# Local attention and a two-layer feed-forward on one core: one written order for units 16 to 127, seven products from unit 20 on, and relu slopes split between ScalarE and VectorE

## The chip, the cores and the metric

The kernel runs on 1 core of one Trainium2 chip. The metric is the device time of one execution in microseconds (us); three runs of the kernel before gave 884.85, 886.47 and 890.36, median 886.47.

## What is computed

Attention with a window of 32 positions and 32 global tokens, 8 batches of 8 heads, 512 local positions, head size 64; its output, 4608 tokens of 512 numbers, goes through a feed-forward of 2048 hidden units with a slope for negative values:

```python
s_g = scale * q_g @ concat(k_g, k_l).T;  out_g = softmax(s_g) @ concat(v_g, v_l)
s_l = concat(scale * q_l @ k_g.T, where(|i - j| <= 32, scale * q_l @ k_l.T, -1e9))
out_l = softmax(s_l) @ concat(v_g, v_l)
x = concat(out_g, out_l) as (4608, 512)
h = x @ w_in                                   # 512 -> 2048
g = maximum(h, 0) + alpha * minimum(h, 0)      # alpha of 2048
return g @ w_out                               # 2048 -> 512
```

## The kernel before

The tokens are nine groups: eight local ones of 512 tokens (one a batch) and one of the 256 global tokens. The hidden layer is cut into 16 blocks of 128. A unit t = 16 G + f is block f of group G: a first product (x by block f of w_in, into a PSUM bank h_ps), the slopes, and, two units later (LAG), the second product (g by block f of w_out, into four banks o). All 32-bit operands are split into an upper part (a cast on ScalarE: xh, gh, wt) and a lower part (a subtraction: xl, gl), and each product is three matmuls, so that a unit of a local group has twelve matmuls of 512 columns in its first product and twelve in its second. Attention is computed beside it, 32 head pairs P, four steps s each, one step a unit: s = 0 local scores (s_ps) and softmax, s = 1 a transpose of the probabilities p through DRAM (transpose_q, fetch_pt), s = 2 values (o_ps and g_ps, two banks), global scores and global softmax, s = 3 the global part's transpose. Group G needs head pairs 4G to 4G + 3.

Units 0 to 15 (begin, line 996) follow an order that a planner at build time writes from costs and due times (early, line 159). The change leaves it alone.

From unit 16 on the loop at the end of longformer_ffn sets the order, in three forms:
- Units 16 to 29 (slow_unit): plain products; ScalarE, VectorE and GpSimd aren't pinned, so the framework's scheduler may move their instructions. CATCH (line 45) gives units 16, 23 and 30 two steps of attention instead of one.
- Units 30 and 31 (border_units): pinned, written out.
- Units 32 to 127 (fast_unit): pinned, "seven products". For two blocks f and f + 1 and the two halves of the tokens, f1_fast (line 831) takes seven products of 256 columns instead of eight, with sums of the weights (weight_sums, line 396: s24, s3 and a changed part of wt) and sums of x (x_sums, line 735, and x_last for group 7: b11, b12, b21, b22 are the quarters of x, t1 to t4 their sums). Four products stand in the even unit, three in the odd one; VectorE then adds the parts (u<-u,h_ps and h_ps<-u,h_ps). The third product of the odd unit reads t4.

The x sums of a group are made at the end of the group before, at the places (f, where) in X_STEPS (line 46); the last step, which makes t4, stands in the group's first unit. The weight sums are made once for each pair q of blocks; six of the eight stand in units 18 to 28, the last two in units 29 and 33.

The slopes of a local unit in units 16 to 127 are two instructions on VectorE (slopes, line 903: g = min(h, 0) alpha, then max(h, 0) + g), but for the last pair of a group (added and both), where ScalarE takes relu(-h) (negatives, line 887) and VectorE adds beta times it to h (add_slopes, line 892), with beta = 1 - alpha (line 1023). Then ScalarE casts gh and GpSimd makes gl.

Banks: h_ps has two buffers, and the attention's s_ps, o_ps and g_ps share two. global_bank (line 556) clears a corner of the g_ps bank with a memset on VectorE before TensorE may write there. Instructions on one engine run in their written order.

Of the kernel before, what the change touches and what calls it, by code (L numbers as in the profile page):

```python
# [7 lines left out]
F32 = mybir.dt.float32  # L8
# [26 lines left out]
HP = 50  # L35
NPRE = 19
# [266 lines left out]
def longformer_ffn(ctx: ExitStack, tc: tile.TileContext, qk, v, w, alpha, out):  # L303
# [82 lines left out]
    def load_out_weights(T):  # L386
        wos[T] = wpool.tile([128, 2, 512], F32R, tag="w", name="wo")
        sync.dma_start(wos[T].bitcast(F32), wod[T % NF])
# [342 lines left out]

    def less(o, a, b):
        vec.tensor_tensor(o, a, b, op=ALU.subtract)

    def x_sums(G, step):
        if step == 0:
            upper(G, "b11", b11)
            lower(G, "b11", b11, vec)
            less(b11, b12, b11)
        if step == 1:  # L740
            less(b12, b22, b12)
        if step == 2:
            upper(G, "t1", b11)
            upper(G, "t3", b12)
# [17 lines left out]
    def x_last(step):  # L762

        G = NB - 1
        if step == 0:
            upper(G, "b11", b11)
            lower(G, "b11", b11, vec)
            less(b11, b12, b11)
            less(b12, b22, b12)
        if step == 1:  # L770
            spare("t2")
            upper(G, "t1", b11)
            upper(G, "t3", b12)
            lower(G, "t1", b11, vec)
        if step == 2:
            less(b11, b22, b11)
            lower(G, "t3", b12, vec)
        if step == 3:
            upper(G, "t2", b11)
            upper(G, "b22", b22)  # L780
            upper(G, "b21", b21)
            lower(G, "t2", b11, vec)
        if step == 4:
            lower(G, "b22", b22, pool)
            lower(G, "b21", b21, vec)
        if step == 5:
            less(b21, b21, b11)
            upper(G, "t4", b21)
            lower(G, "t4", b21, pool)

    def prepare(t, at):
        G, f = divmod(t, NF)
        if f:
            G += 1
        if G == NB - 1 and (f, at) in LAST_STEPS:
            x_last(LAST_STEPS.index((f, at)))
        if G * NF not in FAST or (f, at) not in X_STEPS:
            return
        if G < NB - 1:
            x_sums(G, X_STEPS.index((f, at)))  # L800
# [24 lines left out]
    def product(dst, w, x, start):  # L825
        for c in range(2):
            for j, e in ((0, 0), (1, 0), (0, 1)):
                matmul(dst, w[:, j, 128 * c : 128 * c + 128], x[e][:, 256 * c : 256 * c + 256], start=start, stop=not start, skip_group_check=True)
                start = False

    def f1_fast(T):
        G, f = divmod(T, NF)
        q = f // 2
# [28 lines left out]
        def even():  # L862
            vec.tensor_tensor(h0[:, hi], u[:, lo], h0[:, hi], op=ALU.add)
            prelu(T - 1, h0, SL)

        def odd():
            vec.tensor_tensor(h1[:, lo], u[:, lo], h1[:, lo], op=ALU.add)
            prelu(T, h1, SL)

# [13 lines left out]
        if f == NF - 1:  # L883
            return added, both
        return even, odd
# [6 lines left out]
    def add_slopes(T, g, h):  # L892
        f = T % NF
# [9 lines left out]
    def slopes(T, h, n):  # L903
        f = T % NF
# [73 lines left out]

    def values(P, first):
        last = gpart.pop(P)  # L980
        if live(P - 1):
            ob = bank(first, "o_ps")
            pv_all(P - 1, ob, last)
        if live(P):
            global_scores(P)
        if live(P - 1):
            pv_out(P - 1, ob, last)
# [127 lines left out]
    def attn(u, where):  # L1115
        P, s = divmod(u, 4)
        if not (live(P) or live(P - 1)):
            return
        if (s, where) == (0, "pre") and live(P):
            local_scores(P)  # L1120
        if s < 2 and where == "pre" and live(P):
            part = softmax(P, s)
            part["red"]()
            part["ex"]()
            tails.extend(part[k] for k in ("rza", "rzr", "nm"))
        if where == "mid":
            while tails:
                tails.pop(0)()
        if (s, where) == (2, "mid"):
            gpart[P] = global_bank(P)  # L1130
            values(P, "s")
            if live(P):
                load_v(P)
        if not live(P):
            return
        if (s, where) == (2, "post"):
            global_softmax(P)
            if live(P + 2):
                load_qk(P + 2)
        if P >= NRAW:  # L1140
            if (s, where) == (2, "pre") and (P, 0) not in scratch:
                transpose_q(P, 0)
            if u == NPRE + 2 * NF + len(CATCH) - 1 and where == "post":
                transpose_q(P, 0)
            if (s, where) == (3, "pre") and P > 8:
                fetch_pt(P, 0)
                transpose_q(P, 1)
# [203 lines left out]
```

## Time and profile before

| what | value |
|---|---|
| median of three runs | 886.47 us |
| the profiled execution | 887.61 us |
| its span, first to last instruction | 885.8 us |
| granted TensorE clock | 1.0 |
| TensorE busy (matmuls) | 866.2 us, 98% |
| VectorE busy | 616.3 us, 70% |
| ScalarE busy | 392.7 us, 44% |
| GpSimd busy | 323.9 us, 37% |

The page names the engines PE (TensorE), DVE (VectorE), ACT (ScalarE), POOL (GpSimd) and SP (SyncE). A share is a mean over stages; a matmul's end is modelled, so the time that TensorE takes is read from the distance between starts. Nearly every instruction stands under one line, 294 or 323, since two helpers record them all; tiles tell them apart.

### The profile page before, as it was taken

How to read it: one execution, taken by the hardware profiler on the slowest of the kernel's cores; microseconds unless marked ns; L12 is line 12 of the kernel's file. 1: busy time of each engine (PE TensorE's matmuls, PEld its weight loads, DVE VectorE, ACT ScalarE, POOL GpSimd, SP SyncE). 2: the span in 40 equal slices, each digit the busy share in tenths (PEclk: the TensorE clock that was granted, in tenths of full speed). 3: DMA queues.
4: the chain of work that ended last, by engine and by line, in shares of the span. 5: the costliest groups of instructions: out<-in, count | busy, mean ns of one | idle time of the engine just before them, and what ended most of it. 6: DMA issues, size and time to landing. Idle time of an engine off the chain costs nothing.

```text
span 885.8 us, 22467 instructions
## 1 busy us (share of the span) xinstructions
PE 866.2 (98%) x8678; PEld 751.2 (85%) x8678; DVE 616.3 (70%) x1690; ACT 392.7 (44%) x1162; POOL 323.9 (37%) x281
## 2 busy tenths in 40 slices
PE   7799999999999999999999999999999999999998
PEld 5677777878888888888898888888898898889898
DVE  7999999976767667666676667666676656455432
ACT  7898885544444334432354334432354324211221
POOL 4455443655434332423243332423243323222222
PEclk9999999999999999999999999999999999999999
DMA  9879997977457766776657666776657553645630
GB/s 357 343 256 387 335 336 251 324 247 236 152 180 220 250 214 220 263 241 232 211 173 254 211 215 217 255 250 231 212 184 250 173 185 95 215 168 169 220 134 25
DMA packets 80906, 201.23 MB, mean 227 GB/s; under 512 B 21280, under 2 KB 41248, under 8 KB 77088
## 3 DMA queue, kind: packets, MB, share of 16 engines
q1 hardware_dynamic: 80800, 199.80, 66.1%
q8 instruction: 69, 1.13, 0.5%
q14 instruction: 37, 0.30, 0.1%
HBM read 160.96 MB, written 38.80 MB: 226 GB/s over the span
## 4 chain that ended last, share of the span: by engine, by line
PE 73%; DVE 14%; DMA 6%; ACT 4%; issue 2%; POOL 1%; SPq 1%; DVEq 0%; ACTq 0%; POOLq 0%
PE o L323 34%; PE h_ps L323 30%; PE o_ps L323 4%; PE s_ps L323 3%; DVE wt L294 2%; PE g_ps L323 2%; DVE wsum L294 2%; DVE p L294 2%; DVE g L294 2%; ACT p L294 2%; DVE wraw L294 1%; DMA pt<-scratch 1%; DMA scratch<-p 1%; DMA v<-in_v_dram 1%; DMA wa<-wt 1%
## 5 line engine op out<-in xcount | busy, mean ns | idle before, releaser
L294 POOL TENSOR_TENSOR gl<-g,gh 128x512 fp32r<-128x512 f32 (+1 forms) x128 | 161.4, 1263 | 368.0 <-ACT gh L294 270.4
L323 PE MATMUL o<-gh,wo 128*128 128x512 f32 (+1 forms) x1024 | 244.4, 380 | 0.0
L323 PE MATMUL h_ps<-xh,wt 128*128 128x256 f32 (+1 forms) x1024 | 222.4, 310 | 2.2 <-DVE g L294 1.3
L294 ACT CAST gh<-g 128x512 fp32r<-128x512 f32 (+1 forms) x144 | 85.9, 597 | 289.0 <-DVE g L294 288.3
L323 PEld LDWEIGHTS o<-gh,wo 128*128 128x128 f32 x1024 | 176.7, 188 | 32.1 <-issue 0.4
L323 PEld LDWEIGHTS h_ps<-xh,wt 128*128 128x128 f32 x1024 | 166.2, 188 | 20.5 <-issue 4.0
L323 PE MATMUL h_ps<-xl,wt 128*128 128x256 f32 (+1 forms) x512 | 157.4, 307 | 0.0
L323 PE MATMUL o<-gl,wo 128*128 128x512 f32 (+1 forms) x512 | 131.2, 377 | 0.0
L294 DVE TENSOR_SCALAR g<-h_ps,alpha_sb 128x512 f32<-128x512 f32 (+1 forms) x116 | 82.5, 712 | 39.0 <-PE h_ps L323 33.6
L323 PEld LDWEIGHTS o<-gl,wo 128*128 128x128 f32 x512 | 92.8, 188 | 18.5
L294 POOL TENSOR_TENSOR p<-p,rz 128x512 f32<-128x512 f32 x64 | 70.7, 1121 | 96.2 <-DVE rz L294 93.4
L323 PEld LDWEIGHTS h_ps<-xl,wt 128*128 128x128 f32 x512 | 96.1, 188 | 5.1
L294 DVE TENSOR_TENSOR h_ps<-u,h_ps 128x256 f32<-128x256 f32 x144 | 61.1, 425 | 50.6 <-PE h_ps L323 48.7
L294 ACT ACTIVATE p<-p,mn 128x128 f32<-128x128 f32 x224 | 86.9, 396 | 5.1 <-DVE mn L294 4.9
L323 PE MATMUL h_ps<-xh,s 128*128 128x256 f32 x480 | 88.6, 280 | 0.4 <-DVE h_ps L294 0.2
L294 DVE TENSOR_TENSOR u<-u,h_ps 128x256 f32<-128x256 f32 x96 | 40.3, 420 | 57.0 <-PE h_ps L323 36.7
L323 PEld LDWEIGHTS h_ps<-xh,s 128*128 128x128 f32 x480 | 75.9, 188 | 4.3 <-ACT xe L294 0.7
L294 DVE SCALAR_TENSOR_TENSOR g<-h_ps,g 128x512 f32<-128x512 f32 (+1 forms) x116 | 75.9, 654 | 3.8
L323 PE MATMUL h_ps<-xl,s 128*128 128x256 f32 x240 | 67.1, 279 | 0.0
L294 POOL TENSOR_TENSOR wt<-wt,wr 128x512 int32<-128x512 int32 x32 | 45.4, 1423 | 52.4 <-DVE wt L294 35.0
L323 PEld LDWEIGHTS o_ps<-pt,v 128*64 128x64 f32 x1600 | 49.7, 138 | 8.2 <-issue 2.7
L323 PE MATMUL o_ps<-pt,v 128*64 128x32 f32 (+1 forms) x1600 | 53.5, 223 | 1.7 <-DMA pt<-scratch 1.0
(102 smaller groups left out, 1137.1 us busy)
## 6 DMA issues: line engine op xcount, KB each, us to landing
wo<-wo SPq DMA_DIRECT2D x128, 512.0 KB, 4.3
v<-in_v_dram SPq DMA_DIRECT2D x29, 1024.0 KB, 5.4
qk<-in_qk_dram SPq DMA_DIRECT2D x30, 672.0 KB, 7.0
wraw<-in_w_dram SPq DMA_DIRECT2D x32, 512.0 KB, 8.4
scratch<-p SPq DMA_DIRECT2D x112, 128.0 KB, 2.8
pt<-scratch SPq DMA_DIRECT2D x28, 512.0 KB, 5.7
wo<-wt SPq DMA_DIRECT2D x16, 512.0 KB, 7.1
out_dram<-ost SPq DMA_DIRECT2D x32, 256.0 KB, 3.5
```

Source lines behind the costliest of these rows:

```text
L294: ins = op(*a, **k)
L323: ins = nc.tensor.matmul(*a, **k)
```

## The change

One function, unit(t), writes the order of units 16 to 127, all pinned; slow_unit, border_units, fast_unit, attn and CATCH go. Attention's step is (t + 20) mod 4 in each unit. At unit 16 that is the step it had; the three extra steps are gone, so that from unit 32 on a step stands two units later than before. Units 16 to 19 stay plain (f1_plain, half of the slopes on ScalarE); from unit 20 on f1_fast runs. The x of group 1 is split already, so x_second reuses the split for b11, b21 and b22 and makes t1 to t4 in units 16, 17 and 20. The weight sums of a pair start in the units of FIRSTS (two sums) and end in those of RESTS (four sums, three casts, three low parts); since pairs 0 and 1 come last, group 2 takes its blocks from block 4 on (hidden). The slopes of every seven-product pair now go by added and both. Group 7 uses x_sums too; the difference b12 is taken in two halves, since its second head pair arrives two units later.

```diff
-FAST = range(2 * NF, NB * NF)
-CATCH = (16, 23, 30)
+PLAIN = NF + 4
+FIRSTS = {17: 2, 19: 3, 21: 4, 23: 5, 25: 6, 27: 7, 33: 0, 37: 1}
+RESTS = {18: 2, 20: 3, 22: 4, 24: 5, 26: 6, 28: 7, 34: 0, 38: 1}
-LAST_STEPS = [(12, "post"), (13, "mid"), (13, "post"), (14, "mid"), (14, "post"), (15, "mid")]
+LATE = 4
...
+    def x_second(step):
+        if step == 0:
+            less(b11, b12, b11)
+            less(b12, b22, b12)
+            upper(1, "t1", b11)
+            upper(1, "t3", b12)
+        if step == 1:
+            xs[1, "b11"], xs[1, "b21"], xs[1, "b22"], xs[1, "t4"] = halves(0, 0), halves(2, 0), halves(2, 1), halves(0, 1)
+            lower(1, "t1", b11, vec)
+            less(b11, b22, b11)
+            upper(1, "t2", b11)
+            lower(1, "t3", b12, vec)
+            less(b21, b21, b11)
+            lower(1, "t2", b11, vec)
+        if step == 2:
+            for c in range(2):
+                act.copy(xs[1, "t4"](0, c), x_raw[:, 2 + c, 0:256])
+                pool.tensor_tensor(xs[1, "t4"](1, c), x_raw[:, 2 + c, 0:256], xs[1, "t4"](0, c).bitcast(F32), op=ALU.subtract)
...
     def x_sums(G, step):
         if step == 0:
             upper(G, "b11", b11)
             lower(G, "b11", b11, vec)
+        if step == 1:
             less(b11, b12, b11)
-        if step == 1:
-            less(b12, b22, b12)
+            one_half(b12, b22, b12, 0)
         if step == 2:
             upper(G, "t1", b11)
+            lower(G, "t1", b11, vec)
+            one_half(b12, b22, b12, 1)
+            less(b11, b22, b11)
+        if step == 3:
             upper(G, "t3", b12)
-            lower(G, "t1", b11, vec)
-        if step == 3:
-            less(b11, b22, b11)
             upper(G, "t2", b11)
...
-        if f == NF - 1:
-            return added, both
-        return even, odd
+        return added, both
+
+    def f1_plain(T):
+        h = f1(T, True)
+        def half():
+            us["below"] = negatives(h)
+        def whole():
+            g = us.pop("below")
+            add_slopes(T, g, h)
+            upper_g(T, g, SL)
+            lower_g(T, g, SL)
+        return half, whole
...
-    def fast_unit(t):
-        P, s = divmod(steps[t][0], 4)
+    def unit(t):
+        P, s = divmod(t + 20, 4)
...
-        one, two = f1_fast(t)
+        one, two = f1_plain(t) if t < PLAIN else f1_fast(t)
...
             two()
+            if t == NF:
+                x_second(0)
+            if t == PLAIN:
+                x_second(2)
+            if t in RESTS and s == 0:
+                late.pop(RESTS[t])()
             prepare(t, "mid")
...
             two()
+            if t == NF + 1:
+                x_second(1)
             prepare(t, "mid")
             if s == 1 and live(P):
                 transpose_q(P, 0)
             if s == 3 and live(P):
                 fetch_pt(P, 1)
+            if t in FIRSTS:
+                late[FIRSTS[t]] = weight_sums(FIRSTS[t], True)
         f2(t - LAG, 0)
...
         f2(t - LAG, 1)
+        if t in RESTS and s == 2:
+            late.pop(RESTS[t])()
...
-        if NF <= t < 2 * NF and t % 2 == 0:
-            store_a21((t - NF) // 2)
+        if NF <= t < NF + NF // 2:
+            store_a21((2, 3, 4, 5, 6, 7, 0, 1)[t - NF])
```

VectorE before, from behind the scores' reduction of unit 16 to the transposes of the probabilities, as the scheduler left it (wsum and wt are weight sums and split weights, rz the softmax's divisor):

```order
L294 TENSOR_TENSOR wsum<-wsum 128x256
L294 MEMSET g_ps 64x32
L294 TENSOR_TENSOR wsum<-wsum 128x256 x3
L294 TENSOR_SCALAR g<-h_ps,alpha_sb 128x512
L294 TENSOR_TENSOR wsum<-wt 128x512 x2
L294 SCALAR_TENSOR_TENSOR g<-h_ps,g 128x512
L294 RECIPROCAL rz<-rz 128x4 x2
L294 TENSOR_TENSOR wsum<-wsum 128x256 x4
L294 STREAM_TRANSPOSE p<-p 128x512 x2
```

VectorE now, from behind the same reduction to the memset of unit 18 (x_raw is attention's output, xl a lower part of x):

```order
L293 SCALAR_TENSOR_TENSOR g<-g,beta_sb,h_ps 128x512
L293 TENSOR_TENSOR x_raw<-x_raw 128x2x256 x2
L293 RECIPROCAL rz<-rz 128x4 x2
L293 SCALAR_TENSOR_TENSOR g<-g,beta_sb,h_ps 128x512
L293 TENSOR_TENSOR xl<-x_raw,xh 128x512
L293 TENSOR_TENSOR x_raw<-x_raw 128x2x256
L293 TENSOR_TENSOR xl<-x_raw,xh 128x512
L293 TENSOR_TENSOR x_raw<-x_raw 128x2x256
L293 TENSOR_TENSOR xl<-x_raw,xh 128x512
L293 STREAM_TRANSPOSE p<-p 128x512 x2
L293 TENSOR_TENSOR wsum<-wt 128x512 x2
L293 MEMSET g_ps 64x32
```

The memset of the global bank stood second, ahead of two slopes and the transposes; it stands last now, behind the slopes of units 16 and 17, the x sums of group 1, the transposes and the first two weight sums.

ScalarE before, at the border from group 3 to group 4 (units 63 and 64): casts of x (xh), the relus and casts of the pair's slopes (g, gh), the copy of a sum (u), the cast of t4, and attention's output:

```order
L294 CAST xh<-x_raw 128x512 x2
L294 ACTIVATE g<-h_ps 128x512 x2
L294 CAST xh<-x_raw 128x512
L294 CAST gh<-g 128x512 x2
L294 CAST xh<-x_raw 128x512 x2
L294 COPY u<-h_ps 128x256
L294 CAST xh<-x_raw 128x512
L294 COPY x_raw<-o_ps 128x384
```

ScalarE now, at the same border (p,z are the exponentials of a softmax and their sums):

```order
L293 CAST xh<-x_raw 128x512
L293 ACTIVATE g<-h_ps 128x512 x2
L293 CAST xh<-x_raw 128x512 x2
L293 CAST gh<-g 128x512 x2
L293 CAST xh<-x_raw 128x512 x2
L293 COPY u<-h_ps 128x256
L293 ACTIVATE p,z<-p,mn 128x4x32 x8
L293 ACTIVATE rz<-z 128x4 x2
L293 CAST xh<-x_raw 128x512
```

The cast of t4, the last row, followed the copy of u directly; eight exponentials and two small instructions stand between them now.

## Rows read from the trace of the kernel before

**Rows 1.** The page: span, part 1 (busy us, share of the span, instructions), and VectorE's line of part 2 (busy tenths in 40 slices).
```profile
span 885.8 us, 22467 instructions
...
PE 866.2 (98%) x8678; PEld 751.2 (85%) x8678; DVE 616.3 (70%) x1690; ACT 392.7 (44%) x1162; POOL 323.9 (37%) x281
...
DVE  7999999976767667666676667666676656455432
```

**Rows 2.** Busy time by stretch: stretch in us from the span's start, its length, then PE, PEld, DVE, ACT and POOL busy us (instructions), granted clock, share of the DMA engines, GB/s.
```profile
147.40:179.00 31.60, 31.60 (x313) 25.46 (x314) 30.68 (x67) 15.07 (x44) 16.97 (x15) 1.00 0.89 311
...
400.00:500.00 100.00, 100.00 (x1070) 88.91 (x1069) 67.67 (x199) 40.83 (x129) 32.88 (x28) 1.00 0.67 223
```

**Rows 3.** Timeline of TensorE: start us, length us, engine, line, operation, out<-in, shape, count, and in brackets idle time before it and what ended it. First products of units 16, 17 and 18 (starts), the second product between, the values of unit 18; two places of the seven-product form; the values at 284 us.
```profile
147.39 0.74 PE L323 MATMUL h_ps<-xh,wt 128*128 128x512 f32 x2 [0.56 <-DVE g L294]
...
154.32 0.62 PE L323 MATMUL h_ps<-xh,wt 128*128 128x512 f32 x2
...
157.07 1.99 PE L323 MATMUL o<-gh,wt 128*128 128x512 f32 x8
...
159.82 0.62 PE L323 MATMUL h_ps<-xh,wt 128*128 128x512 f32 x2
...
162.66 1.59 PE L323 MATMUL o_ps<-pt,v 128*64 128x32 f32 x48
164.08 0.66 PE L323 MATMUL g_ps<-pt,v 128*64 128x32 f32 x16
...
284.02 0.69 PE L323 MATMUL g_ps<-pt,v 128*64 128x32 f32 x16 [0.69 <-DVE g_ps L294]
...
404.18 0.40 PE L323 MATMUL h_ps<-xh,wt 128*128 128x256 f32 x2
...
406.65 0.40 PE L323 MATMUL h_ps<-xh,s 128*128 128x256 f32 x2
```

**Rows 4.** Groups of instructions by form over the whole span, slopes: line, engine, operation, out<-in, shapes, count | busy us, mean ns of one | idle us before them and what ended it.
```profile
L294 DVE TENSOR_SCALAR g<-h_ps,alpha_sb 128x512 f32<-128x512 f32 x100 | 74.8, 748 | 7.2 <-PE h_ps L323 1.9 <-DMA out_dram<-ost 0.6
...
L294 DVE SCALAR_TENSOR_TENSOR g<-h_ps,g 128x512 f32<-128x512 f32 x100 | 69.1, 691 | 3.2
...
L294 DVE SCALAR_TENSOR_TENSOR g<-g,beta_sb,h_ps 128x512 f32<-128x512 f32 x28 | 20.3, 742 | 1.0 <-ACT g L294 1.0
...
L294 ACT ACTIVATE g<-h_ps 128x512 f32<-128x512 f32 x28 | 16.6, 592 | 15.8 <-DVE h_ps L294 13.8 <-PE h_ps L323 1.8
```

**Rows 5.** Timeline of VectorE from the low parts (gl) of units 14 and 15 over the reduction of unit 16 (CUSTOM, the first of eight) to the transposes, and at 281 us.
```profile
150.38 1.28 DVE L294 TENSOR_TENSOR gl<-g,gh 128x512 fp32r<-128x512 f32 x2
...
152.25 1.28 DVE L294 TENSOR_TENSOR wsum<-wt 128x512 f32<-128x512 f32 x2
...
154.05 0.28 DVE L294 CUSTOM_DVE_ANT_0 p<-s_ps,mask 128x128 f32<-128x128 f32 x1
...
155.74 0.72 DVE L294 TENSOR_TENSOR wsum<-wsum 128x256 f32<-128x256 f32 x1
...
158.41 2.84 DVE L294 TENSOR_TENSOR wsum<-wt 128x512 f32<-128x512 f32 x2
...
166.01 1.29 DVE L294 STREAM_TRANSPOSE p<-p 128x512 f32<-128x512 f32 x2
...
281.21 2.60 DVE L294 TENSOR_TENSOR wsum<-wsum 128x256 f32<-128x256 f32 x4
283.88 0.09 DVE L294 MEMSET g_ps<- 64x32 f32 x1
```

**Rows 6.** Timelines of ScalarE (first and last of the eight exponentials of unit 16) and of GpSimd beside the weight sums of rows 5.
```profile
154.69 0.40 ACT L294 ACTIVATE p<-p,mn 128x128 f32<-128x128 f32 x1
...
157.40 0.39 ACT L294 ACTIVATE p<-p,mn 128x128 f32<-128x128 f32 x1
...
158.96 2.89 POOL L294 TENSOR_TENSOR s<-wsum,s 128x512 fp32r<-128x512 f32 x2
162.01 2.37 POOL L294 TENSOR_TENSOR p<-p,rz 128x512 f32<-128x512 f32 x2 [0.16 <-DVE rz L294]
```

**Rows 7.** Timelines at the border of group 4 (units 64 and 65): VectorE's last split and the difference for t4, ScalarE's cast, GpSimd's low part, and the start of the product that reads it.
```profile
458.58 0.68 DVE L294 TENSOR_TENSOR xl<-x_raw,xh 128x512 fp32r<-128x512 f32 x1
459.30 0.69 DVE L294 TENSOR_TENSOR x_raw<-x_raw 128x512 f32<-128x512 f32 x1
...
460.03 0.62 ACT L294 CAST xh<-x_raw 128x512 fp32r<-128x512 f32 x1 [4.08 <-DVE x_raw L294]
...
460.73 1.29 POOL L294 TENSOR_TENSOR xl<-x_raw,xh 128x512 fp32r<-128x512 f32 x1 [2.28 <-ACT xh L294]
...
463.66 0.40 PE L323 MATMUL h_ps<-xh,wt 128*128 128x256 f32 x2
```

**Rows 8.** Timelines of a unit with scores (unit 62) and the odd unit behind it: the scores, the odd unit's third product, VectorE's last sum, ScalarE's copy of u and its small instructions behind the exponentials.
```profile
442.33 1.16 PE L323 MATMUL s_ps<-qk 64*32 64x128 f32 x64
...
450.51 0.40 PE L323 MATMUL h_ps<-xh,wt 128*128 128x256 f32 x2
...
447.53 0.43 DVE L294 TENSOR_TENSOR h_ps<-u,h_ps 128x256 f32<-128x256 f32 x1
...
445.19 0.37 ACT L294 COPY u<-h_ps 128x256 f32<-128x256 f32 x1 [1.63 <-PE h_ps L323]
...
448.55 0.34 ACT L294 ACTIVATE rz<-z 128x4 f32<-128x4 f32 x2
```

More of the change, by code (lines that the diff above doesn't have):

```diff
@@ L387, in load_out_weights @@
         wos[T] = wpool.tile([128, 2, 512], F32R, tag="w", name="wo")
-        sync.dma_start(wos[T].bitcast(F32), wod[T % NF])
+        sync.dma_start(wos[T].bitcast(F32), wod[hidden(T)])
     def load_a21(q):
@@ L760, in x_sums @@
             lower(G, "t4", b21, pool)
[L762 to L789, printed above, removed]
     def prepare(t, at):
@@ L794, in prepare @@
             G += 1
[L795 to L799, printed above, removed]
+        if 2 <= G < NB and (f, at) in X_STEPS:
             x_sums(G, X_STEPS.index((f, at)))
@@ L827, in product, with hidden @@
             for j, e in ((0, 0), (1, 0), (0, 1)):
-                matmul(dst, w[:, j, 128 * c : 128 * c + 128], x[e][:, 256 * c : 256 * c + 256], start=start, stop=not start, skip_group_check=True)
+                piece = x(e, c) if callable(x) else x[e][:, 256 * c : 256 * c + 256]
+                matmul(dst, w[:, j, 128 * c : 128 * c + 128], piece, start=start, stop=not start, skip_group_check=True)
                 start = False
+    def hidden(T):
+        G, f = divmod(T, NF)
+        return (f + LATE) % NF if G == 2 else f
     def f1_fast(T):
         G, f = divmod(T, NF)
-        q = f // 2
+        q = hidden(T) // 2
         x = lambda name: xs[G, name]
@@ L892, in add_slopes @@
     def add_slopes(T, g, h):
-        f = T % NF
+        f = hidden(T)
         vec.scalar_tensor_tensor(g, g, beta_sb[:, f : f + 1], h, op0=ALU.mult, op1=ALU.add)
@@ L903, in slopes @@
     def slopes(T, h, n):
-        f = T % NF
+        f = hidden(T)
         g = stage("g")
@@ L977, in longformer_ffn @@
     gpart = {}
[L979 to L987, printed above, removed]
     def values_pe(P):
@@ L1113, in begin @@
             issue(name)
[L1115 to L1147, printed above, removed]
-            if (s, where) == (3, "post") and P > 8:
-                fetch_pt(P, 1)
@@ L1151, in longformer_ffn @@
-    tails = []
     begin()
     pin_sync[0] = False
-    steps = [[] for t in range(NT + LAG)]
-    u = NPRE + NF
-    for t in range(NF, NT + LAG):
-        steps[t] = [u, u + 1] if t in CATCH else [u]
-        u = steps[t][-1] + 1
-    def attention(t, at):
-        with tc.high_priority(offset=HP):
-            if len(steps[t]) == 1:
-                attn(steps[t][0], at)
-                return
-            order = [(k, a) for k in range(2) for a in ("pre", "mid", "post")]
-            i = 2 * ("pre", "mid", "post").index(at)
-            for k, a in order[i : i + 2]:
-                attn(steps[t][k], a)
@@ L1222, in fast_unit @@
             parts = [softmax(P, h) for h in range(2)]
-        if s == 2 and (live(P) or live(P - 1)) and P not in gpart:
+        if s == 2 and (live(P) or live(P - 1)):
             gpart[P] = global_bank(P)
-        one, two = f1_fast(t)
+        one, two = f1_plain(t) if t < PLAIN else f1_fast(t)
         if f % 2 == 0:
@@ L1264, in fast_unit @@
         f2(t - LAG, 1)
+        if t in RESTS and s == 2:
+            late.pop(RESTS[t])()
+    late = {}
     load_out_weights(NF)
@@ L1268, in longformer_ffn @@
         G, f = divmod(t, NF)
-        pin[0] = t in FAST or t in (2 * NF - 2, 2 * NF - 1)
-        if t in FAST:
-            fast_unit(t)
-        elif pin[0]:
-            border_units(t)
-        else:
-            slow_unit(t)
+        pin[0] = t < NB * NF
+        if pin[0]:
+            unit(t)
+        else:
+            if t < NT:
+                f1(t)
+            f2(t - LAG, 0)
+            f2(t - LAG, 1)
         prepare(t, "post")
```

65 lines of the change are left out of this document (6 added, 59 removed).

## The prediction

> **What bounds the kernel now.** I read the page first: TensorE is busy 866.2 of 885.8 us, VectorE 616.3 [rows 1]. The digits of VectorE by slice show 9 at the very start and in the slices around 140 us, and 6 or 7 for most of the rest. The table by stretches says the same sharply: from 147.4 to 179 us TensorE is busy all 31.60 us and VectorE 30.68 of them; from 400 to 500 us TensorE is busy all 100 us, VectorE 67.67, ScalarE 40.83, GpSimd 32.88 [rows 2]. So behind unit 16 TensorE sets the time, and only two things can help: fewer columns through it, or less of its idle time. Of idle time there is little: the timeline of TensorE has 0.56 us before unit 16 (a bank not yet read by VectorE) and 0.69 us at 284 us (the memset of a global bank comes late) [rows 3]; nothing of that size stands behind 300 us.
>
> The profiled execution took 887.61 us, of which 885.8 are the span; the median of the three timed runs is 886.47. I make the sum against 887.61 and carry the difference over to the median.
>
> **What the change removes from TensorE.** A plain unit runs twelve products of 512 columns, from 154.32 to 157.07 us: 2.75 us, 5.50 a pair. Seven products are 42 matmuls of 256 columns; 21 of them start between 404.18 and 406.65, which is 117.6 ns each, 4.94 us a pair [rows 3]. Six pairs (units 20 to 31) change form: 6 x 0.56 = 3.4 us. It is off the bound engine, so it counts in full. The two idle stretches should go too: the scores now stand ahead of unit 16's products and give VectorE 1.16 us for the bank that was 0.56 late, and at 284 us the four sums that stood before the memset go behind unit 34. That is 1.25 more: a gain of 4.65 us together.
>
> **The slopes.** A unit of local slopes costs VectorE 748 + 691 ns; now it is 592 ns on ScalarE and 742 ns on VectorE [rows 4]. Four units take some 25 us, so VectorE loses 2.8 us and ScalarE gains 2.4 of each 25. Both have that room between 400 and 500 us [rows 2], TensorE has no idle time there to give back, and the banks are read earlier than now. I put it at 0. It can't be below that; if ScalarE's exponentials ever stood before the relu in a busy stretch, it would be a wait of the kind priced below.
>
> **What it adds, first place: the memset of unit 18.** VectorE's queue is now the written order. Between the scores' reduction of unit 16 and the memset of unit 18 stand the new sums of x for group 1 (two differences, then three splits and two differences), two transposes, and the first two sums of weights; before, the scheduler had put that memset ahead of most weight sums. TensorE can't start the values' second bank (g_ps) before the memset. I walk it with the trace's durations.
> TensorE: the scores start where unit 16's products were to start, at 146.8; 1.1 us on, 2.75 of products, 2.75 of second products (157.07 to 159.82), so unit 17 starts at 153.4, unit 18 at 158.9, its products end at 161.6, and 1.42 us later (162.66 to 164.08) it wants the bank [rows 3]: 163.05.
> VectorE: the low parts of units 14 and 15 end at 151.6; the reduction takes 1.7 (154.05 to 155.74); slope 0.7 and two differences 1.4 bring it to 155.4 [rows 4, 5]. Then it waits for ScalarE, whose exponentials take 3.0 us (154.69 to 157.70) and start at 151.9; behind them stand the sum's two small ones, a cast, two casts of x and only then the relu of unit 17: 157.6 [rows 6]. The slope ends at 158.3. The five x instructions are 3.2 us when nothing disturbs them. But GpSimd then works on the probabilities and on a low part, some 2.6 us of overlap, and the trace shows what that does: the same two weight sums took 1.28 us at 152.25 and 2.84 at 158.41, while GpSimd ran two of its own from 158.96 [rows 5, 6]. At that rate 2.6 us hold 1.2 us of work, so the x instructions end at 162.9, the transposes (1.2 us) at 164.1, the weight sums at 165.4, and the memset behind them. TensorE waits 2.3 us. Bounds: 0 if ScalarE's relu comes first in practice and GpSimd is done, 3.5 with no work in the overlap.
> The Trainium skill (SBUF — State Buffer, section Who interferes with whom) says that a VectorE instruction with two SBUF inputs and a GpSimd instruction that reads SBUF take one read port by turns, each for its whole length. By that rule all 2.6 us of overlap are lost, this wait is 3.5 and the total below 1.2 us more; the lengthening in the row, 1.56 us beside 2.89 us of GpSimd, lies between that and none.
>
> **Second place: units 20 to 28.** Weight sums (4.3 us of VectorE for each of six) now share their units with three sums and two slopes. By the durations above VectorE has about 22 us of work in each four units, against some 24.6 us of TensorE. In unit 21 the transposes wait for GpSimd, which has low parts of x and weights before the probabilities; the two weight sums and the memset of unit 22 follow. The trace has exactly this case: four sums of 2.60 us stood before the memset at 283.88 and cost 0.69 [rows 3, 5]. I take one such wait at unit 22, 0.8 us with the unit's margins, nothing at 26 and 30 where GpSimd has less; bounds 0 and 3.
> The eight stores of the weights' first halves go out in units 16 to 23 instead of every second unit to 30: four more of 256 KB in a stretch where the DMA engines are busy to 0.89 [rows 2]. What waits on that queue, a unit's output weights, is wanted two units later: 0.
>
> **Third place: the borders of groups 2 to 6.** Attention no longer catches up three steps, so from unit 32 on it stands two units later against the groups. A group's first unit now holds scores and their eight exponentials; before, it held values. In that unit the last split of x (t4) is made: difference on VectorE, cast on ScalarE, low part on GpSimd. Before, at unit 64, the difference ran 459.30 to 459.99, the cast started 460.03, the low part 460.73 and ended 462.02; TensorE came to that product at 463.66 [rows 7]: 1.9 us to spare. The unit with scores as it is now, 442.33 to 449.1, shows the new place: VectorE's three sums end at 447.96, ScalarE copies from 445.19 and is done with the exponentials at 448.9, and TensorE starts the third product of the next unit at 450.51 and wants the low part two matmuls later, at 450.74 [rows 8]. Into it go: reduction and sums 0.2 later (two splits stand before them), a split 0.72 and the difference 0.69 (458.58 to 459.99): 449.55. From there to the end of the low part 2.05 us as at 459.99 to 462.02: 451.6. TensorE waits 0.9 us. Five borders have scores in their first unit (groups 2 to 6): 4.5 us. Bounds: 0 if the scores' reduction runs beside the products and the x work is no later than now, 1.4 each where GpSimd's other low parts lengthen VectorE's: 0 to 7. Group 7's border has no scores left: 0.
>
> **The sum.** -3.4 - 1.25 + 2.3 + 0.8 + 4.5 = +2.95 us: 890.6 beside 887.61, and 889.4 beside the median. A measurement of this kernel (884.85 to 890.36 in three runs) tells about 1%, 8.9 us, from no change: the limits are 877.6 and 895.3.
>
> **The rivals.**
> All waits hidden: the written order holds, as the slack of VectorE at 400 to 500 us suggests (a third of it idle), and only the 4.65 us count: 881.8. Against it speaks the 0.69 at 284 us, the very wait that the new order makes likelier. Chance 0.3. It would be faster by 0.5%, and no step takes it past 1%, since TensorE has no idle time left to lose.
> VectorE becomes the bound in units 17 to 28: every two-input instruction there (12 sums of 0.64 us, 24 of 0.41, 7 of x at 0.65: 22 us) meets GpSimd and takes 2.2 times as long, as at 158.41. The 26 us more are swallowed up to the idle time that VectorE would have (some 15 us in twelve units), so about 10 us stand on TensorE; with the borders it is -4.65 + 10 + 4.5: 896.3, slower by 1.1%. It decides as soon as two memsets in a row are late by more than 2 us. For it: VectorE at 30.68 of 31.60 [rows 2]; against: TensorE didn't wait in that stretch although VectorE was full. By the rule of SBUF — State Buffer named above this is the likelier of the two rivals in the stretch of weight sums. Chance 0.15.
> The borders cost nothing but unit 18 and 22 do: -4.65 + 3.1, 884.9. It lies in my own case.
>
> **How the numbers follow.** The forecast, waits that eat the gain, has 0.55. Its own range by the bounds: 2.3 from 0 to 3.5, 0.8 from 0 to 3, 4.5 from 0 to 7. All low is 881.8, all high 895.3 with the gain in full. I take 881 to 896: the first rival's value is in, about half of the second. Faster by over 1%: 0.03 (only spread between runs); slower by over 1%: 0.13 (half of the second rival, and 0.05 from the upper end of my own case); within: 0.84.
>
> **What would show it.** TensorE's plain matmuls of 512 columns into h_ps fall from 384 to 240 and the span of a pair in units 20 to 31 from 5.50 to 4.94. TensorE idle before g_ps by VectorE's g_ps, 2.3 us in unit 18 and 0.8 in unit 22; idle before the third product of units 33, 49, 65, 81 and 97 by GpSimd's xl, 0.9 each; none of this at unit 113. The forecast is wrong if those five waits are missing (then 885 or less), or if TensorE waits more than 5 us between units 17 and 30.

## The result, and the profile after

The changed kernel takes 894.52 us (median of seven runs, 891.46 to 897.22); the kernel before takes 887.09 beside it (seven runs, 884.85 to 890.36). The ratio is 1.009, 95% interval 1.0069 to 1.011: slower by 0.9%. The forecast was 889.4 in a range of 881 to 896, and "within 1%".

The profiled execution after took 891.46 us, the fastest of its seven, and 3.85 more than that of before (887.61). Its page, span and part 1, beside [rows 1]: TensorE 3.8 us less busy in a span that is 3.9 longer, VectorE 51 less, ScalarE 63 more.

```profile
span 889.7 us, 22792 instructions
...
PE 862.4 (97%) x8786; PEld 752.5 (85%) x8786; DVE 565.1 (64%) x1633; ACT 455.7 (51%) x1273; POOL 322.8 (36%) x283
```

Where TensorE's idle time stands: groups by form, first matmuls that wait, with idle us before them and what ended it. Before, the first group had none and the second 0.7.

```profile
L322 PE MATMUL h_ps<-xl,wt 128*128 128x256 f32 x432 | 120.5, 279 | 4.7 <-POOL xl L293 4.7
...
L322 PE MATMUL g_ps<-pt,v 128*64 128x32 f32 x224 | 15.0, 219 | 4.4 <-DVE g_ps L293 4.4
```

Both waits of the forecast are there: TensorE stands idle 4.4 us for late memsets and 4.7 us for the low part of t4. This is the idle time behind the modelled end of a matmul; what a wait costs, read from starts, is more; the section on the prediction prices it. The timeline of TensorE at unit 18, and at unit 22:

```profile
162.21 1.59 PE L322 MATMUL o_ps<-pt,v 128*64 128x32 f32 x48
166.06 1.12 PE L322 MATMUL g_ps<-pt,v 128*64 128x32 f32 x16 [2.26 <-DVE g_ps L293]
...
168.07 2.70 PE L322 MATMUL o<-gh,wo 128*128 128x512 f32 x8
...
171.52 0.62 PE L322 MATMUL h_ps<-xh,wt 128*128 128x512 f32 x2
...
194.27 0.69 PE L322 MATMUL g_ps<-pt,v 128*64 128x32 f32 x16 [1.20 <-DVE g_ps L293]
...
195.36 2.12 PE L322 MATMUL o<-gh,wo 128*128 128x512 f32 x8
...
198.23 0.40 PE L322 MATMUL h_ps<-xh,s 128*128 128x256 f32 x2
```

From the start of g_ps to the next unit's first product is the same work in both units. It takes 3.96 us at unit 22 (194.27 to 198.23) and 5.46 at unit 18 (166.06 to 171.52): 1.5 us more. The reason is in the table by stretches (columns as in [rows 2]; the granted clock is the number before the DMA share): the clock is at half, the lower of its two levels (1.2 GHz), from the wait of 2.26 us to the middle of 169:170. Of before, the same column is 1.00 from 147 us on. The last row answers to the second of [rows 2].

```profile
163.00:166.00 3.00, 0.81 (x30) 0.69 (x24) 3.00 (x7) 0.71 (x2) 0.00 (x0) 0.99 0.90 324
166.00:167.00 1.00, 0.94 (x18) 0.94 (x20) 0.59 (x2) 0.38 (x1) 0.00 (x0) 0.50 0.36 83
...
168.00:169.00 1.00, 1.00 (x4) 0.83 (x3) 0.49 (x2) 0.27 (x1) 0.65 (x1) 0.50 1.18 213
169.00:170.00 1.00, 1.00 (x5) 0.78 (x4) 0.48 (x3) 0.43 (x2) 0.00 (x0) 0.81 0.60 205
170.00:171.00 1.00, 1.00 (x6) 0.84 (x5) 0.76 (x4) 0.24 (x3) 0.00 (x0) 1.00 0.94 393
...
400.00:500.00 100.00, 99.16 (x1064) 87.78 (x1063) 58.43 (x186) 48.85 (x143) 31.88 (x26) 1.00 0.66 222
```

VectorE and GpSimd ahead of that memset (timelines; answers to [rows 5, 6]):

```profile
157.81 0.75 DVE L293 SCALAR_TENSOR_TENSOR g<-g,beta_sb,h_ps 128x512 f32<-128x512 f32 x1 [1.87 <-ACT g L293]
158.48 0.69 DVE L293 TENSOR_TENSOR xl<-x_raw,xh 128x512 fp32r<-128x512 f32 x1
159.20 1.41 DVE L293 TENSOR_TENSOR x_raw<-x_raw 128x512 f32<-128x512 f32 x1
160.54 1.78 DVE L293 TENSOR_TENSOR xl<-x_raw,xh 128x512 fp32r<-128x512 f32 x1
...
164.67 1.25 DVE L293 TENSOR_TENSOR wsum<-wt 128x512 f32<-128x512 f32 x2
...
165.92 0.09 DVE L293 MEMSET g_ps<- 64x32 f32 x1
...
157.58 2.48 POOL L293 TENSOR_TENSOR p<-p,rz 128x512 f32<-128x512 f32 x2
160.03 1.74 POOL L293 TENSOR_TENSOR gl<-g,gh 128x512 fp32r<-128x512 f32 x1
```

VectorE waits 1.87 us for the relu of unit 17, which ScalarE now makes; one difference takes 1.41 us instead of 0.69 beside GpSimd's p<-p,rz, one split 1.78 instead of 0.69 beside its gl; and the memset stands last. (The row of 157.58 holds two multiplications; the second begins at 158.58.)

The border of group 4 (answers to [rows 7]): the last difference ends at 462.30, the cast follows at 462.33, GpSimd's low part ends at 464.30, and TensorE has stood for 0.84 us.

```profile
461.61 0.69 DVE L293 TENSOR_TENSOR x_raw<-x_raw 128x512 f32<-128x512 f32 x1
...
462.33 0.62 ACT L293 CAST xh<-x_raw 128x512 fp32r<-128x512 f32 x1 [0.62 <-DVE x_raw L293]
...
463.03 1.27 POOL L293 TENSOR_TENSOR xl<-x_raw,xh 128x512 fp32r<-128x512 f32 x1 [2.57 <-ACT xh L293]
...
461.53 0.40 PE L322 MATMUL h_ps<-xh,s 128*128 128x256 f32 x2
...
464.35 0.39 PE L322 MATMUL h_ps<-xl,wt 128*128 128x256 f32 x1 [0.84 <-POOL xl L293]
...
464.94 2.00 PE L322 MATMUL o<-gh,wo 128*128 128x512 f32 x8
```

From start to start the odd unit's product takes 3.41 us here (461.53 to 464.94); in the odd units without a wait it takes 2.04 or 2.12. So a border costs 1.3 us, more than its idle time.

The slopes by form (answers to [rows 4]): 128 units now go half on ScalarE, at the lengths that they had.

```profile
L293 DVE SCALAR_TENSOR_TENSOR g<-g,beta_sb,h_ps 128x512 f32<-128x512 f32 x128 | 92.5, 746 | 10.6 <-ACT g L293 9.8
L293 ACT ACTIVATE g<-h_ps 128x512 f32<-128x512 f32 x128 | 75.2, 596 | 131.1 <-DVE h_ps L293 124.4 <-PE h_ps L322 3.5
```

### The profile page after: what moved, and what is told of

It is laid out like the page before. It is cut to its first block, busy times and chain, and to the rows that moved or that the text cites. A ratio compares the mean times of both kernels' runs of the same rounds, so it can differ in the third digit from the quotient of the medians.

```text
span 889.7 us, 22792 instructions
## 1 busy us (share of the span) xinstructions
PE 862.4 (97%) x8786; PEld 752.5 (85%) x8786; DVE 565.1 (64%) x1633; ACT 455.7 (51%) x1273; POOL 322.8 (36%) x283
## 4 chain that ended last, share of the span: by engine, by line
PE 69%; DVE 12%; DMA 6%; ACT 5%; POOL 4%; issue 3%; SPq 1%; DVEq 0%; POOLq 0%; ACTq 0%
PE o L322 32%; PE h_ps L322 28%; PE o_ps L322 4%; PE g_ps L322 3%; PE s_ps L322 3%; DMA pt<-scratch 2%; DVE wt L293 2%; POOL xl L293 2%; DMA wraw<-in_w_dram 2%; ACT p L293 1%; DVE p L293 1%; DVE xl L293 1%; POOL gl L293 1%; DVE wraw L293 1%; DMA scratch<-p 1%
## 5 line engine op out<-in xcount | busy, mean ns | idle before, releaser
L322 PE MATMUL h_ps<-xh,wt 128*128 128x256 f32 (+1 forms) x1024 | 209.1, 299 | 1.7 <-DVE g L293 0.9
L322 PE MATMUL h_ps<-xl,wt 128*128 128x256 f32 (+1 forms) x512 | 151.9, 297 | 4.7 <-POOL xl L293 4.7
L293 ACT ACTIVATE g<-h_ps 128x512 f32<-128x512 f32 x128 | 75.2, 596 | 131.1 <-DVE h_ps L293 124.4
L293 DVE TENSOR_TENSOR h_ps<-u,h_ps 128x256 f32<-128x256 f32 x162 | 68.2, 427 | 72.7 <-PE h_ps L322 70.9
L322 PE MATMUL h_ps<-xh,s 128*128 128x256 f32 x552 | 100.0, 278 | 0.0
L293 DVE SCALAR_TENSOR_TENSOR g<-g,beta_sb,h_ps 128x512 f32<-128x512 f32 x128 | 92.5, 746 | 10.6 <-ACT g L293 9.8
L322 PEld LDWEIGHTS h_ps<-xh,s 128*128 128x128 f32 x552 | 87.0, 188 | 3.8
L322 PE MATMUL h_ps<-xl,s 128*128 128x256 f32 x276 | 76.6, 277 | 0.0
L293 DVE CUSTOM_DVE_ANT_0 p<-s_ps,mask 128x128 f32<-128x128 f32 x224 | 49.6, 287 | 27.6 <-PE s_ps L322 27.6
L293 ACT COPY u<-h_ps 128x256 f32<-128x256 f32 x54 | 20.4, 377 | 84.1 <-PE h_ps L322 82.6
```

Of the source, the lines that this page charges most:

```text
L293: ins = op(*a, **k)
L322: ins = nc.tensor.matmul(*a, **k)
```

## The experiments

The theory behind them: the change loses its gain in a few waits of TensorE, each of which has one late instruction on another engine. The rivals: the slopes on ScalarE cost, or the waits come back elsewhere when they are taken away. The first four ran beside each other, with the kernel before at 886.77.

**The slopes alone**, in the kernel before:

```diff
-        if f == NF - 1:
-            return added, both
-        return even, odd
+        return added, both
```

> The kernel before with one part of the change alone: the slopes of all seven-product pairs (units 32 to 127) half on ScalarE. Theory: VectorE's busy time falls by some 55 us and ScalarE's grows by as much, the time stays within 0.5 us of the kernel before, since TensorE has no idle time there. Rival (the slopes make part of the loss): 2 us or more slower, with waits before h_ps or g_ps in each period of four units.

Measured: 886.62, ratio 0.9997 (0.9984 to 1.0011). In units 32 to 127 the slopes cost nothing and bring nothing: VectorE's busy time fell from 616.3 to 556.7 us, ScalarE's grew from 392.7 to 442.5, and the time stayed. The run doesn't touch units 16 to 31, where the relu of unit 17 on ScalarE keeps VectorE waiting 1.87 us ahead of the late memset; that part of the loss is the new slopes' and the order's together.

**The memset a unit earlier**, in the changed kernel, in all units:

```diff
-        if s == 2 and (live(P) or live(P - 1)):
+        if s == 1 and (live(P) or live(P - 1)):
             gpart[P] = global_bank(P)
```

> The changed kernel with one thing moved: the bank of the global scores is taken, and its memset written, at the start of the unit with step 1 instead of step 2, ahead of that unit's x sums, transposes and weight sums. Theory: TensorE's waits before g_ps in units 18, 22, 26 and 30 (2.26 + 1.19 + 0.67 + 0.32 = 4.44 us in the trace of the changed kernel) go, and with them the 3.4 us at half clock that follow the first of them (about 1.2 us), so the profiled span falls from 889.7 to about 884, the clock of every run is 1.0 or nearly, and the median falls by 6 or more from 894.5, since the runs with a lower clock are those that this wait makes. Rival (the clock falls for another reason, such as the waits at the group borders): the median falls by some 4 only and clocks of 0.992 to 0.998 stay. Rival (VectorE as the bound): the waits come back elsewhere in units 17 to 30 and the span stays above 888.

Measured: 887.81, ratio 1.001 (0.9997 to 1.0023). No wait of g_ps is left, the clock stays at 1.0 there, and the five border waits stand at 0.84 as before. Against the kernel before the loss falls from 7.4 to 1.0 us. The profiled span is 887.3 us and not the expected 884, since the wait of 0.21 us before unit 30's first product has grown to 1.06 (the rival's "elsewhere"). Seven of the twelve runs have granted clocks of 0.995 to 0.997; so have runs of the kernel before beside them, and no profile shows where. Timelines of ScalarE, VectorE and TensorE for the new wait:

```profile
232.43 0.62 ACT L293 CAST xh<-x_raw 128x512 fp32r<-128x512 f32 x1
...
233.08 0.75 DVE L293 TENSOR_TENSOR xl<-x_raw,xh 128x512 fp32r<-128x512 f32 x1 [1.82 <-ACT xh L293]
...
236.23 0.48 PE L322 MATMUL h_ps<-xh,wt 128*128 128x256 f32 x2 [1.06 <-DVE g L293]
```

The cast for the first split of group 2, written in unit 28, stands behind three casts of weight sums on ScalarE; VectorE waits for it, and the slopes that read the bank stand behind that split on VectorE.

**t4 in the group before**: the last step of the x sums moved into the step before it.

```diff
             upper(G, "b21", b21)
-        if step == 6:
             lower(G, "b21", b21, vec)
             less(b21, b21, b11)
             upper(G, "t4", b21)
             lower(G, "t4", b21, pool)
```

> The changed kernel with the last step of x_sums (lower part of b21, difference, cast and low part of t4) written at the end of the group before, ahead of the scores' reduction and exponentials of the first unit. Theory: the five waits of 0.85 us before the third product of units 33, 49, 65, 81 and 97 and the 0.43 at unit 113 go (4.7 us), the waits of units 18 to 30 stay, and so does the fall of the clock behind unit 18: span about 885, clocks below 1.0 in part of the runs, median about 890. Rival (the border waits are moved, not removed, since the reduction of the first unit comes 1.4 us later): new waits of about the same sum before the products of units 32, 33 or before the values of unit 34, span 888 to 890.

Measured: 911.16, ratio 1.0287 (1.0257 to 1.0316): a miss by over 20 us. The waits of 0.84 are gone, and before the first product of the same odd units TensorE waits some 2.9 us for VectorE's sum (2.12 at group 7). VectorE, GpSimd and TensorE at the border of group 2:

```profile
258.06 4.10 DVE L293 TENSOR_TENSOR xl<-x_raw,xh 128x512 fp32r<-128x512 f32 x3 [0.17 <-ACT xh L293]
262.19 1.67 DVE L293 TENSOR_TENSOR x_raw<-x_raw 128x512 f32<-128x512 f32 x1
...
258.55 3.06 POOL L293 TENSOR_TENSOR gl<-g,gh 128x512 fp32r<-128x512 f32 x2 [11.49 <-ACT gh L293]
261.58 1.74 POOL L293 TENSOR_TENSOR xl<-x_raw,xh 128x512 fp32r<-128x512 f32 x1
...
266.95 0.47 PE L322 MATMUL h_ps<-xh,s 128*128 128x256 f32 x2 [2.89 <-DVE h_ps L293]
```

Three splits and the difference now meet GpSimd's low parts and take 5.8 us instead of some 2.8 (four of 0.69); the scores' reduction and the sums stand behind them. Half clock comes with three of the five waits of 2.84 to 2.89 us in this profile; the mean granted clock of the runs is 0.976 to 0.989.

**Both edits together:**

> Both moves in one. Theory: nearly no idle time of TensorE behind unit 16 (9.3 us in the changed kernel), no fall of the clock, span about 880 and median about 882, some 0.5% faster than the kernel before: what is left are the six pairs of seven products (3.4 us) and the idle time of the kernel before (1.3 us). Rival (slopes on ScalarE or the later attention cost something by themselves, hidden now behind the waits): median not below 887.

Measured: 904.07, ratio 1.0217 (1.0183 to 1.0251). A miss with the same cause; the early memset is still worth 7 us.

**t4's low part on VectorE**, on top of the early memset. In this comparison the kernel before had 887.95.

```diff
-            lower(G, "t4", b21, pool)
+            lower(G, "t4", b21, vec)
```

> The kernel with the early memset, and the low part of t4 (groups 2 to 7) on VectorE, behind the difference, instead of on GpSimd. Theory (the border wait is the chain difference, cast, GpSimd's low part of 1.27 us): ScalarE's cast ends at 257.73 in that kernel's trace, VectorE would end the low part at 258.4 where GpSimd ends at 259.08, and TensorE wants it at 258.29: five waits fall from 0.84 to about 0.2 us, group 7's 0.43 goes, so 3.6 us less, 884.2. Rival (the wait is moved): VectorE's sum of the odd unit stands behind the low part and comes 0.8 us later, ScalarE's relu with it, and the next unit's first product waits for the bank: no gain or slower, 887.5 to 890.

Measured: 886.34, ratio 0.998 (0.996 to 1.0). ScalarE, VectorE and TensorE at the border of group 4:

```profile
457.58 0.62 ACT L293 CAST xh<-x_raw 128x512 fp32r<-128x512 f32 x1 [0.61 <-DVE x_raw L293]
...
458.23 0.69 DVE L293 TENSOR_TENSOR xl<-x_raw,xh 128x512 fp32r<-128x512 f32 x1 [0.69 <-ACT xh L293]
...
458.98 0.39 PE L322 MATMUL h_ps<-xl,wt 128*128 128x256 f32 x1 [0.22 <-DVE xl L293]
```

The wait falls to 0.22 or 0.23 as worked out, at all five borders, and group 7's 0.43 goes. Against the kernel before on the same chip the gain over the early memset is 1.0 + 1.6 = 2.6 us, where 3.6 were expected.

**The same, and in unit 28 the split ahead of the casts:**

```diff
             vec.tensor_tensor(a12, a12, a11, op=ALU.subtract)
+            if between:
+                between()
...
             if t in RESTS and s == 0:
-                late.pop(RESTS[t])()
-            prepare(t, "mid")
+                late.pop(RESTS[t])(lambda: prepare(t, "mid"))
+            else:
+                prepare(t, "mid")
```

> The same, and in unit 28 the cast and low part of b11 stand between the four weight sums and their casts instead of behind them. Theory (the 1.06 us at 234.8 come from VectorE's low part of b11, which waits 1.82 us for a cast that stands behind three casts of weight sums): that wait goes, 1 us less than with the first edit alone, 883.2, and faster than the kernel before by about 3 us (0.4 per cent). Rival (VectorE is full in that unit and is late anyway): the wait stays near 1 us and the time is that of the first edit alone, 884.2.

Measured: 884.8, ratio 0.9974 (0.9955 to 0.9993): the version that beats both kernels, the one before by 3.2 us (0.3%, its interval just below 1). The 1.06 us are gone; a smaller wait has come for a later split (timeline of TensorE, unit 32):

```profile
254.93 0.38 PE L322 MATMUL h_ps<-xl,s 128*128 128x256 f32 x1 [0.55 <-DVE xl L293]
```

**Only unit 18's memset earlier, beside the changed kernel again** (the kernel before here: 885.44):

```diff
-        if s == 2 and (live(P) or live(P - 1)):
+        if s == (1 if t < NF + 4 else 2) and (live(P) or live(P - 1)):
```

> The changed kernel once more, beside the kernel before on the same chip, for the two edits below. Waits and half clock that its profile showed come to some 3.9 us over the kernel before; its median was 7.4 over. Theory (the traces hold the whole change and the medians scatter from chip to chip): 4 to 5 us over. Rival (runs without a profile have more half clock than the profiled one): 7 over, with lower granted clocks than the kernel before has here.

> The changed kernel with the memset of unit 18's global bank one unit earlier, the others where they are. Theory (the wait of 2.26 us brings the half clock, worth some 1.2 us): both go, 3.4 us less than the changed kernel, and a granted clock of 1.0 between 160 and 175 us. Rival (only the wait counts): 2.3 us less.

Measured: the changed kernel 892.64, ratio 1.0071 (1.0055 to 1.0086), so 7.2 over; with the one memset moved 888.91, ratio 1.0033 (1.0021 to 1.0045), 3.7 less, and its clock stays at 1.0 through the stretch. So one instruction of 0.09 us, written behind bulk work, was half of the loss: 2.3 of wait, and the rest is about the 1.5 of half clock. The changed kernel is 7 over again, the rival's number, but hardly for the rival's reason: the mean granted clock is 0.996 in its runs and 0.997 in those of the kernel before.

**Late memsets in the kernel before**: the memset repeated in eight units. The first EXTRA below is that of the kernel with large counts, the second that of the kernel with small ones.

```diff
+EXTRA = {36: 40, 44: 55, 52: 70, 60: 40, 68: 55, 76: 85, 84: 70, 92: 55}
+EXTRA = {44: 17, 52: 21, 60: 25, 68: 28, 76: 32, 84: 21, 92: 25, 100: 17}
...
             gpart[P] = global_bank(P)
+            for _ in range(EXTRA.get(t, 0)):
+                vec.memset(gbank[P][64:128, 192:224], -3.0e38)
```

> The kernel before, with the memset of the global bank repeated 40, 55, 70, 40, 55, 85, 70 and 55 times more in units 36, 44, 52, 60, 68, 76, 84 and 92, nothing else. At 85 ns each and with the 2.3 us that the memset is early there, the values' second bank should wait 1.1, 2.4, 3.6, 1.1, 2.4, 4.9, 3.6 and 2.4 us, 21.5 together. Theory (TensorE's clock falls to half behind a wait of some 2.3 us, as behind unit 18's): the granted clock shows 0.5 for about 3.4 us behind the six longer ones and not behind the two of 1.1, and each such dip costs some 1.2 us: 21.5 + 7 = 28.5 us over the kernel before, 915. Rival (the dip behind unit 18 came from something else in that stretch): no dips there, 21.5 us over, 908.

> The kernel before, with the memset of the global bank repeated 17, 21, 25, 28, 32, 21, 25 and 17 times more in units 44, 52, 60, 68, 76, 84, 92 and 100. One repetition took 165 ns and the memset was 2.25 us early, so the waits should be 0.6, 1.2, 1.9, 2.4, 3.0, 1.2, 1.9 and 0.6 us, 12.8 together. Theory (the clock falls only behind waits like unit 18's): half clock behind the 2.4 and the 3.0, none behind 0.6 and 1.2 as none stood behind unit 22's 1.19; 12.8 and two to four times 1.2 us make 15 to 18 over the kernel before. Rival (any wait of this size brings it): eight dips, 22 over.

Measured, large counts: 966.13, ratio 1.0878 (1.0845 to 1.091), 78 us over. 915 was expected. Repeated memsets start 167 ns apart, though each lasts 85, so that the waits were 4.3 to 11.7 us, 62.2 together. Half clock comes with all eight, and the work from g_ps to the next unit's first product took 5.55 to 6.45 us instead of 3.94: 16.3 us. 62.2 + 16.3 is 78.5.

Small counts: 905.14, ratio 1.0215 (1.0182 to 1.0248), 19.7 over. TensorE at units 60, 68, 76 and 84, then stretches behind three of them:

```profile
438.23 0.69 PE L324 MATMUL g_ps<-pt,v 128*64 128x32 f32 x16 [1.83 <-DVE g_ps L295]
...
491.61 1.12 PE L324 MATMUL g_ps<-pt,v 128*64 128x32 f32 x16 [2.18 <-DVE g_ps L295]
...
547.05 1.12 PE L324 MATMUL g_ps<-pt,v 128*64 128x32 f32 x16 [3.00 <-DVE g_ps L295]
...
600.17 0.69 PE L324 MATMUL g_ps<-pt,v 128*64 128x32 f32 x16 [1.16 <-DVE g_ps L295]
```

```profile
439.00:444.00 5.00, 5.00 (x20) 3.94 (x17) 3.37 (x11) 1.47 (x4) 0.00 (x0) 0.66 0.77 244
...
492.00:498.00 6.00, 6.00 (x31) 4.71 (x30) 3.06 (x11) 1.47 (x4) 0.00 (x0) 0.52 0.68 246
...
600.00:603.00 3.00, 2.83 (x30) 2.38 (x31) 2.40 (x9) 0.51 (x2) 0.00 (x0) 1.00 0.31 61
```

In this profile half clock comes with the waits of 1.82, 1.83, 2.18 and 3.00 us, and costs 1.5 to 2.9 us each, 8.4 together; none with 0.35, 1.01 and 1.16. Waits 11.7 and half clock 8.4 are 20.1. The profiled execution itself is the slowest of the four, 908.70 and so 23.3 over, with two more stretches of half clock ahead of unit 16. The two fastest (900.0 and 902.37) have mean granted clocks of 0.994 and 0.995 against its 0.985, so not every execution has these dips. The price per dip is above the 1.2 of the theory; the dips are four, since the waits of 1.82 and 1.83 brought one each, and not the rival's eight.

**The kernel before, profiled once more:**

> The kernel before, profiled once more. In its first profile four units of seven products took 24.89 us each time, in that of the slopes alone 24.92 and 24.50 in turn, with a granted clock of 1.0 and no wait in either. Theory (the difference comes with the execution, not with the program, so that the first profile was one of the slower executions of the kernel before and the pair of profiles showed too little of the change's cost): stretches of 24.50 stand in this profile too, some 2 us less behind 260 us than in the first. Rival (the program's order or its buffers set it): 24.89 throughout again.

Measured: 885.46 in one run, with a granted clock of 1.0; a second run of the same program beside it took 888.99 (0.996). The scores (one head pair each, four units apart) in this profile, then in the first profile of before, where the third is 442.33 [rows 8] (the last row counts 58 of 64, since its view ends at 443):

```profile
392.78 1.16 PE L323 MATMUL s_ps<-qk 64*32 64x128 f32 x64
417.28 1.16 PE L323 MATMUL s_ps<-qk 64*32 64x128 f32 x64
442.20 1.06 PE L323 MATMUL s_ps<-qk 64*32 64x128 f32 x58
```

```profile
392.54 1.16 PE L323 MATMUL s_ps<-qk 64*32 64x128 f32 x64
417.44 1.16 PE L323 MATMUL s_ps<-qk 64*32 64x128 f32 x64
```

24.50 and 24.92 us here, 24.90 and 24.89 there. Matmuls of 256 columns are 113.3 ns apart in the short stretches and 117.8 in the others. So, as far as two executions can show, this comes with the execution and not with the program, as the theory had it, and the first profile is the longer of the two, by 2.15 us. Behind 293 us all of its stretches are long ones; sixteen of them take 3.1 us more than the same sixteen here.

## Why the prediction was right, and which step of it failed

Sign, verdict and mechanism held: waits of the written order eat the gain. The size did not: the forecast was 2.9 us over the kernel before, the medians say 7.4, and the range's width took in the rest. By its steps, from the profiled pair, once by TensorE's idle time and once by what is lost from start to start (the same work with and without the wait):

| term | predicted | idle time | by starts |
|---|---|---|---|
| seven products in units 20 to 31 | -3.4 | | -3.7 |
| old waits gone | -1.25 | -1.9 | -3.0 |
| unit 18's memset | +2.3 | +2.26 | +2.4 |
| units 20 to 30 | +0.8 | 1.20 + 0.67 + 0.21 + 0.32 = +2.4 | +3.1 |
| borders of groups 2 to 6 | 0.9 x 5 = +4.5 | 0.84 x 5 = +4.2 | 1.3 x 5 = +6.5 |
| border of group 7 | 0 | +0.43 | +0.7 |
| half clock behind unit 18's wait | none | | +1.5 |
| matmuls of units 32 to 127 closer together | none | | -3.4 |
| sum | +2.95 | | +4.1 (the pair: +3.85) |

**Products.** In units 20 to 31 the matmuls of 256 columns stand 116.0 ns apart, those of 512 columns before 228.9: 4.87 us a pair instead of 5.49. The step was right.

**Closer matmuls.** In units 32 to 127 the matmuls of 256 columns stand 117.0 ns apart in before's profile and 115.3 in after's, over some 2060 distances 3.4 us. The change isn't the cause, for the kernel before has 115.7 in its second profile. This scatter hid almost half of the loss in the pair.

**Unit 18.** The walk came out to 0.04 us, by errors that cancel: the bank was wanted at 163.8, not 163.05, and the memset came at 165.92, not behind 165.4. Beside GpSimd the x instructions lost 1.8 us where 1.4 were forecast: 0.7 in the difference at 159.20 and 1.1 in the split at 160.54. By the rule of the Trainium skill (SBUF — State Buffer, Who interferes with whom), one holder of the shared port at a time, the order of issue decides which of the two blocks. The trace agrees: the difference began while GpSimd ran p<-p,rz and ended 0.55 us behind its end, the split began while GpSimd ran gl and ended 0.55 behind that; and where VectorE's split at 158.48 came first, GpSimd's multiplication of 158.58 took 1.48 us instead of 1.04. So the prediction's "all 2.6 us of overlap are lost" put on VectorE alone what both engines paid.

**Units 20 to 30.** The step "one such wait at unit 22, 0.8 with the unit's margins, nothing at 26 and 30" failed in its second half. At units 22 and 26 two weight sums of 2.38 us stand ahead of the memset, at unit 30 two differences of x of 2.24; ahead of them the transposes wait for GpSimd, 2.27, 1.97 and 0.72 us, so less work on GpSimd only halves the wait each time. The bound, 3, held by idle time (2.4) and not by starts (3.1).

**Borders.** As a wait the step for groups 2 to 6 is right to 0.06 each; as a price it is 0.4 short, since idle time is counted from a matmul's modelled end and the matmuls beside the wait are spread too (two stand 0.23 us apart instead of 0.12). "Group 7's border has no scores left: 0" is wrong in its reason: what covered the chain before were the values and global scores between the first unit's products and the odd unit's, 2.5 us of TensorE (456.88 to 459.37 at group 4 before). Without them the chain difference, cast, low part is late by itself, 0.43; where scores and their exponentials stand in the unit too, it is 0.84.

**The missed term.** I priced a wait at its own length. Behind the longest one TensorE worked at half clock, and the runs above show that this came with the wait: the late memsets bring it in the kernel before, and the early one takes it away. It isn't certain: with waits of 1.82 to 3.00 us it comes in 13 of 19 cases in the five profiles with such waits (in all seven where TensorE waited for a memset, in 4 and in 2 of the six at the borders of the two kernels with t4 in the group before), and two of the changed kernel's 13 runs (893.17 and 889.52 us) have a mean granted clock of 1.0.

**What is left of the median.** The pair shows 3.85 us, the medians 7.4 and 7.2. Against the second profile of before (885.46) the changed kernel's profile is 6.0 over. Without the row of closer matmuls, which belongs to the execution, the terms by starts make +7.5. That the medians show this sum is an estimate: runs without a profile show no distances.

**The rivals.** "All waits hidden" (881.8) was wrong. "VectorE becomes the bound" (896.3) is nearest to the median, 1.8 us off where the forecast is 5.1 off. Its mechanism holds in one place: from 158 to 166 us VectorE is busy 7.96 of 8.00 us, ahead of unit 18's memset. From 178 to 255 us it is busy 58.7 of 77, and late behind single instructions. Between units 17 and 30 TensorE is idle 4.7 us, just under the five that the forecast named as its own limit; by starts it loses 5.5.

## What to carry to other kernels

Where one engine sets the time, a written order costs by its latest small instruction: look in each unit at what the bound engine waits for and put that ahead of the bulk work on its engine (here a memset of 0.09 us was worth 3.7 us). Price a wait from starts, not from idle time (here 1.3 us for an idle 0.84), and one of TensorE of 2 us or so at about twice its length, since half clock came in 13 of 19 cases and cost 1.5 to 2.9 us where it was measured. Before a small difference is read from one pair of profiles, compare the distances of the same matmuls in both (here 3.4 us of scatter hid almost half of the loss). When work leaves a place, ask what it covered: the values that moved away had hidden a chain over three engines, and moving the head of that chain earlier made it collide with GpSimd, where shortening it (one engine fewer) worked.

## What the runs showed of the hardware

- The granted clock fell to half in or right behind 13 of 19 waits of 1.82 to 3.00 us, with none of 1.51 us and shorter (all from 141 us on), and with all eight of 4.3 us and more.
- With the granted clock at 1.0, the same matmuls of 256 columns follow each other in 113.3 or 117.8 ns for a stretch of units; which it is changed between two executions of the kernel before. What decides it stays open. Over the 16 stretches from 293 to 690 us it was worth 3.1 us.
- Back-to-back memsets on one corner of a PSUM bank last 85 ns each, as a single one does, and start 167 ns apart.
- VectorE's subtraction of two SBUF tiles (128 x 512) takes 0.69 us alone. Begun while GpSimd multiplied p by rz it took 1.41, begun while GpSimd made gl 1.78, and each ended 0.55 us behind GpSimd's instruction; begun 0.10 us ahead of a GpSimd multiplication it kept 0.69, and that one took 1.48 instead of 1.04.
